# Linear attention followed by a multiplicative FFN on one core: q, k and v spread over 128 partitions, 64x64 array tiles for the small products, and a written-out order of all steps

## The chip, the core and the metric

The kernel runs on one NeuronCore of a Trainium2 chip. A core has a matrix engine (PE in the profile; PEld are its weight loads), a vector engine (DVE), an activation engine (ACT), a general engine (POOL) and a queue processor that issues DMAs (SP). The metric is the device time of one execution in microseconds (us), as the median of several runs. Smaller is better.

## What is computed

```python
# q, k, v: (8 batches, 8 heads, 576 tokens, 64); x becomes (4608 tokens, 512)
q_s = softmax(q, axis=-1)            # over the 64 channels
k_s = softmax(k, axis=2)             # over the 576 tokens
kv  = einsum('bhsd,bhse->bhde', k_s, v)      # one 64x64 matrix per head
x   = einsum('bhsd,bhde->bhse', q_s, kv)     # then heads beside each other: 4608 x 512
out = (((x @ w1) * (x @ w2)) @ w3) @ w_out   # 512 -> 1024, 1024 -> 1024 -> 512
```

Inputs and outputs are float32; the products run in float16.

## The kernel before

**Weights.** `make_w3o` casts `w_out` and `w3` to float16, transposes the blocks of `w3` on PE (line 439) and multiplies them (line 453), so that `w3 @ w_out` is one 1024x512 matrix `W3O`. `make_w12` casts `w1` and `w2` and makes the sums of their quadrants (`wc`, line 476) that the seven-product scheme below needs.

**Attention of one batch (`attention`).** k and v arrive with 64 groups of 9 tokens x 2 heads on 128 partitions, two loads of 576 KB each (line 246 issues every load). q arrives in another layout: 96 partitions of 6 tokens, pool `sq` with 2 buffers. ACT takes the exponentials (k at line 298, q at line 316). DVE sums q's rows and takes reciprocals (lines 322 and 324), POOL normalises q (line 327) and casts v (line 305). q is then transposed to `qsT`: for batches 0 and 1 on PE (line 342, copied out by DVE at line 348), for the others by a transposing DMA (line 354). The product kv runs in 64x64 array tiles, two at a time on the diagonal of the array: head i uses partitions 64i to 64i+63 and writes PSUM partitions 64i to 64i+63 (line 370, 72 matmuls of 65 columns for a batch; column 65 is the sum of k's exponentials). DVE takes reciprocals (line 377) and writes the normalised kv of two heads as a block diagonal 128x128 matrix `kv2` with two instructions (line 380). The x product is then 8 full-array matmuls of 288 columns (line 396), copied into `xt` by ACT (line 410; half of batch 0 by DVE). PSUM holds `pa` (2 banks, attention), `px` (2) and `pp` (4).

**FFN.** Tokens are cut into groups: one of 512 tokens done plainly (`plain`, lines 508, 515, 521) and five of 640, 896, 896, 896 and 768 tokens, whose two first products are done with a seven-product scheme on halves (`wino`): `t_comb` makes sums of x's quadrants on DVE (line 543), then for each of 8 blocks of 128 features there are 14 matmuls of h columns, h being half the group (line 567), three evictions by ACT (lines 588, 589), four DVE operations (line 592) and one product on POOL (line 618). `s2` multiplies by `W3O`: 8 matmuls of 512 columns for 128 tokens (line 633), evicted by ACT (line 643) or, every second time in the last group, by DVE (line 645), and stored by SP (line 657).

**What sets the order.** Every step is a task with an engine, an assumed duration, dependencies, buffers, a priority and a class. `Planner.run` plays the tasks through with the assumed durations when the program is built, picks for every engine the task that could start first (ties by class and priority), gives buffers out, and puts filler matmuls on a blank tile (line 712) where PE would stand idle in the first 65 us. The order it finds is the program order of each engine; on the chip each engine works through its list strictly in that order and waits at a step whose inputs are late.

Of the kernel before, what the change touches and what calls it, by code (L numbers as in the profile page):

```python
# [14 lines left out]

class Buf:


    def __init__(self, pool):
        self.pool, self.users, self.tile, self.left = pool, [], None, 0  # L20


class Task:
    def __init__(self, eng, dur, emit, deps, bufs, prio, cls, dma):
        self.eng, self.dur, self.emit, self.prio, self.cls, self.dma = eng, dur, emit, prio, cls, dma
        self.deps = [d for d in deps if d is not None]
        self.bufs = bufs
        self.start = self.done = None


class Fill:


    def __init__(self, op, tile, n):
        self.op, self.tile, self.n = op, tile, n

    def emit(self):
        self.op(self.tile, self.n)


class Planner:

    LAT = {"PE": 230, "ACT": 150, "DVE": 150, "POOL": 150, "SP": 60}

    def __init__(self):
        self.tasks, self.pools = [], {}
        self.filler = None

    def pool(self, name, tiles):
        self.pools[name] = [(0.0, i, t) for i, t in enumerate(tiles)]

    def add(self, eng, dur, emit, deps=(), bufs=(), prio=0.0, cls=1, dma=None):
        t = Task(eng, dur, emit, list(deps), list(bufs), prio, cls, dma)
        for b in t.bufs:
            b.users.append(t)
            b.left += 1
        self.tasks.append(t)
        return t  # L60

    def run(self):
        engines = ["PE", "ACT", "DVE", "POOL", "SP"]
        todo = {e: sorted((t for t in self.tasks if t.eng == e), key=lambda t: t.prio)
                for e in engines}
        free = {e: 0.0 for e in engines}
        asleep = {e: False for e in engines}
        dma_free = 0.0
        order = []

        def ready(t):
            r = 0.0
            for d in t.deps:
                if d.done is None:
                    return None
                r = max(r, d.done)
            need = {}
            for b in t.bufs:
                if b.tile is None:
                    need[b.pool] = need.get(b.pool, 0) + 1  # L80
            for p, n in need.items():
                have = sorted(self.pools[p])
                if len(have) < n:
                    return None
                r = max(r, have[n - 1][0])
            return r

        while any(todo.values()):
            best = None
            for e in engines:  # L90
                if not todo[e]:
                    continue
                t0 = free[e]
                cands = []
                seen = 0
                for t in todo[e]:
                    r = ready(t)
                    if r is not None:
                        cands.append((max(r, t0), t))
                    seen += 1  # L100
                    if seen >= (400 if e == "PE" else 200):
                        break
                if not cands:
                    continue
                first = min(c[0] for c in cands)

                slack = 0 if e == "PE" else 120
                now = [c for c in cands if c[0] <= first + slack]
# [5 lines left out]
                if best is None or s < best[0]:  # L114
                    best = (s, e, t)
# [630 lines left out]
```

## Time and profile before

| | |
|---|---|
| runs | 259.37, 256.09 and 259.29 us; median 259.29 |
| span of the profiled execution | 257.3 us from its first to its last instruction |
| PE busy | 234.6 us (91%) |
| DVE, ACT, POOL busy | 175.7, 151.8 and 109.4 us |
| DMA | 52.10 MB, 38.80 MB of it read from memory by the inputs |

The profile is one execution, and only its span is listed; the median of the runs lies 2.0 us above that span, for what lies around it (and for the spread of the runs). A busy PE in the profile includes the drain of each matmul, which overlaps the next one, so busy PE isn't PE at its peak: the distance from one matmul's start to the next is the better measure. The "DMA share" is the mean busy share of 16 DMA engines by packet time and can pass 1. In the groups, a line shows out<-in, shapes, the number of instructions, busy time and mean ns, and then the idle time of the engine just before them with what ended it.

### The profile page before, as it was taken

The numbers are of one execution on the slowest core, as the hardware profiler recorded it, in microseconds if no ns is written. First come the engines' busy times: TensorE is split into PE (matmuls) and PEld (weight loads), VectorE is DVE, ScalarE is ACT, GpSimd is POOL, SyncE is SP. The second block draws the span as 40 slices with busy tenths as digits, with TensorE's granted clock in tenths as the row PEclk, the third lists the DMA queues.
The fourth block names the chain that finished last, engine by engine and source line by source line (L and its number), as shares of the span: only waits on it lengthen the run. The fifth ranks groups of instructions, "written<-read, shape, count | busy, mean of one in ns | idle before, by whom it ended". The sixth has DMA issues, their size and how long they took to land.

```text
span 257.3 us, 5030 instructions
## 1 busy us (share of the span) xinstructions
PE 234.6 (91%) x1820; PEld 126.5 (49%) x1820; DVE 175.7 (68%) x331; ACT 151.8 (59%) x312; POOL 109.4 (43%) x103
## 2 busy tenths in 40 slices
PE   8999889969689989699799797999999999999991
PEld 5755644443356644444455354554444455555440
DVE  2448399958787797897988979956657464565321
ACT  1147447937678979489598696655355544444310
POOL 3025800467644678367957582713132222221200
PEclk9999999997999999799999999999999999999998
DMA  7999999999979799999999951232211313122254
GB/s 256 404 328 348 399 383 286 356 209 360 220 210 383 101 307 311 334 261 292 274 293 181 381 134 46 48 85 72 50 43 42 82 41 84 41 52 71 63 149 118
DMA packets 41945, 52.10 MB, mean 202 GB/s; under 512 B 16832, under 2 KB 27072, under 8 KB 41920
## 3 DMA queue, kind: packets, MB, share of 16 engines
q1 hardware_dynamic: 41920, 51.79, 70.0%
q8 instruction: 14, 0.23, 0.4%
q14 instruction: 11, 0.09, 0.1%
HBM read 38.80 MB, written 9.44 MB: 187 GB/s over the span
## 4 chain that ended last, share of the span: by engine, by line
PE 55%; DVE 18%; DMA 15%; ACT 5%; issue 4%; SPq 1%; DVEq 0%; ACTq 0%
PE pp L633 19%; PE px L567 16%; PE pp L567 12%; DMA st<-in_moe_w_dram 10%; DVE tt L543 4%; DMA sq<-in_q_dram 4%; DVE ds L322 4%; DVE c L592 4%; PE pp L712 4%; PE pa L396 3%; DVE kv L380 2%; DMA out_dram<-osb 2%; DVE ab L592 1%; ACT xt L410 1%; ACT eq L316 1%
## 5 line engine op out<-in xcount | busy, mean ns | idle before, releaser
L633 PE MATMUL pp<-W3O,ab 128*128 128x512 f16 x288 | 80.8, 384 | 0.3 <-DVE c L592 0.2
L618 POOL TENSOR_TENSOR ab<-c,c 128x448 f16<-128x448 f16 (+2 forms) x40 | 39.4, 985 | 81.5 <-DVE c L592 80.4
L592 DVE TENSOR_TENSOR c<-pp,u 128x448 f16<-128x448 f32 (+2 forms) x80 | 46.2, 579 | 29.5 <-ACT u L588 15.7
L327 POOL TENSOR_TENSOR eq<-eq,ds 96x768 f16<-96x768 f16 x32 | 47.1, 1487 | 33.9 <-DVE ds L324 25.6
L567 PEld LDWEIGHTS <-wc 128*128 128x128 f16 x320 | 30.6, 98 | 35.2 <-DVE tt L543 4.9
L567 PE MATMUL px<-tt,wc 128*128 128x448 f16 (+2 forms) x160 | 40.2, 339 | 3.8 <-DVE tt L543 3.6
L633 PEld LDWEIGHTS <-ab 128*128 128x128 f16 x288 | 28.2, 98 | 26.4 <-issue 2.9
L588 ACT COPY u<-px 128x448 f32<-128x448 f32 x48 | 26.0, 546 | 17.9 <-PE px L567 13.6
L643 ACT ACTIVATE osb<-pp 128x512 f32<-128x512 f32 x33 | 19.7, 614 | 25.7 <-PE pp L633 23.4
L567 PEld LDWEIGHTS <-w 128*128 128x128 f16 x240 | 23.3, 98 | 22.1 <-issue 2.3
L322 DVE TENSOR_REDUCE ds<-eq 96x12 f32<-96x768 f16 x32 | 29.6, 925 | 3.9 <-ACT eq L316 3.8
L316 ACT ACTIVATE eq<-sq 96x768 f16<-96x768 f32 x32 | 26.0, 842 | 7.9 <-DMA sq<-in_q_dram 7.9
L410 ACT CAST xt<-pa 128x288 f16<-128x288 f32 (+6 forms) x72 | 23.0, 380 | 12.6 <-PE pa L396 12.5
L592 DVE TENSOR_TENSOR c<-pp,s 128x448 f16<-128x448 f32 (+2 forms) x40 | 23.0, 578 | 8.5 <-PE pp L567 7.6
L592 DVE TENSOR_TENSOR ab<-px,c 128x448 f16<-128x448 f32 (+2 forms) x40 | 23.3, 582 | 4.3 <-PE px L567 2.0
L589 ACT COPY u<-px 128x320 f32<-128x320 f32 (+1 forms) x32 | 14.2, 452 | 12.9 <-PE px L567 8.7
L567 PE MATMUL px<-xt,wc 128*128 128x448 f16 (+2 forms) x80 | 20.2, 335 | 1.2 <-ACT u L589 1.2
L567 PE MATMUL pp<-tt,wc 128*128 128x448 f16 (+2 forms) x80 | 20.4, 336 | 0.8 <-DVE tt L543 0.5
L298 ACT ACTIVATE ek<-st 128x576 f16<-128x576 f32 x32 | 21.0, 691 | 0.0
L567 PE MATMUL pp<-xt,w 128*128 128x448 f16 (+2 forms) x80 | 20.8, 342 | 0.0
L567 PE MATMUL pp<-tt,w 128*128 128x448 f16 (+2 forms) x80 | 20.3, 336 | 0.3 <-DVE c L592 0.3
L567 PE MATMUL px<-xt,w 128*128 128x448 f16 (+2 forms) x80 | 20.0, 336 | 0.2 <-DVE ab L592 0.2
(55 smaller groups left out, 254.3 us busy)
## 6 DMA issues: line engine op xcount, KB each, us to landing
sq<-in_q_dram SPq DMA_DIRECT2D x16, 576.0 KB, 8.5
st<-in_k_dram SPq DMA_DIRECT2D x16, 576.0 KB, 7.9
st<-in_v_dram SPq DMA_DIRECT2D x16, 576.0 KB, 8.7
st<-in_moe_w_dram SPq DMA_DIRECT2D x16, 512.0 KB, 7.7
out_dram<-osb SPq DMA_DIRECT2D x24, 192.0 KB, 2.3
out_dram<-osb SPq DMA_DIRECT2D x24, 128.0 KB, 2.4
st<-in_moe_w_out_dram SPq DMA_DIRECT2D x4, 512.0 KB, 7.0
out_dram<-osb SPq DMA_DIRECT2D x24, 64.0 KB, 2.0
```

What stands on the lines that cost most here:

```text
L298: nc.scalar.activation(out=ek.tile.rearrange("p r d -> p (r d)"), in_=vk(bk.tile)[:, g], func=AF.Exp)
L316: nc.scalar.activation(out=eq.tile.rearrange("p r h d -> p h r d"), in_=vq(bq.tile)[:, o:o + 2].rearrange("p h (r d) -> p h r d", r=R), fu ...
L322: nc.vector.tensor_reduce(out=ds.tile[:, 0], axis=AX.X, op=ALU.add, in_=eq.tile.rearrange("p r h d -> p (r h) d"))
L327: nc.gpsimd.tensor_tensor(out=eq.tile.rearrange("p r h d -> p (r h) d"), in0=eq.tile.rearrange("p r h d -> p (r h) d"), in1=ds.tile[:, 1][ ...
L410: (nc.vector.tensor_copy if by_dve else nc.scalar.copy)(out=xt_buf[i].tile[:, p, lo - starts[i]:hi - starts[i]], in_=xp.tile[:, lo - base: ...
L567: nc.tensor.matmul(ps.tile[:, 0:h], lhsT=lhs(c), rhs=rhs(c), start=first and c == 0, stop=c == 1, skip_group_check=not first)
L588: return lambda: nc.scalar.copy(out=dst.tile, in_=src.tile[:, 0:h]) if h == HM else \
L589: nc.scalar.copy(out=dst.tile[:, 0:h], in_=src.tile[:, 0:h])
L592: return lambda: nc.vector.tensor_tensor(out=dst(), in0=ps.tile[:, 0:h], in1=other.tile[:, 0:h], op=op)
L618: nc.gpsimd.tensor_tensor(out=ab.tile[:, 0:h], in0=c11.tile[:, 0:h], in1=c21.tile[:, 0:h], op=ALU.mult)
L633: nc.tensor.matmul(po.tile, lhsT=ab_buf[(i, ft)].tile[:, tb * P:(tb + 1) * P], rhs=W3O[ft], start=(ft == 0), stop=(ft == N_FT - 1))
L643: nc.scalar.activation(out=osb.tile, in_=po.tile, func=AF.Copy, scale=ISC)
```

## The change

**Order.** `Planner` is gone. `Steps` numbers the 1344 tasks in the order in which the code adds them, and two lists written out by hand give everything: `ORDER`, the task numbers in order of issue (six filler entries among them, 90 matmuls in all, where there were 92), and `SLOTS`, the buffer of its pool that each use gets. No durations or priorities are left. Numbers 0 to 67 are the loads (0 to 7 `w3` and `w_out` in turn, 8 and 9 `w3`, 10 to 15 q, k, v of batch 0, 16 and 17 `w3`, 18 to 25 `w1` and `w2`, then q, k, v of batches 1 to 7). Read with this numbering, the loads now begin with 10, 6, 11, 4, 2, 8, 0 (q of batch 0 among the first); the last piece of k of batch 0 is the 17th load and the last of the two loads of `w1` and `w2` that the first feature blocks need is the 24th. Before, batch 0 was complete with the 16th load and those two with the 20th.

**Where products stand in PE's list.** Between the second half of kv of a batch and the first x product of that batch PE's list holds, for batches 0 to 7: 2, 2, 18, 21, 18, 20, 44 and 30 other entries, nearly all of them pairs of matmuls of 320 to 512 columns. Between two neighbouring entries that use the 64x64 tiles (a half of kv or a piece of x) there are at most 3 others in 20 of 53 cases. The first product of a seven-product group stands 3 to 7 entries behind the last x product that it needs.

**Attention.** q is loaded like k and v, on 128 partitions (2 heads x 64 groups of 9 tokens), from one pool `st` of 8 buffers for all loads (before: `st` 7 and `sq` 2). The exponentials write two heads side by side. q's row sums are 4 DVE instructions of 128x576 for a batch (before: 4 of 96x768), with 2 reciprocals (before: 4) and 2 normalisations of 128x1152 on POOL (before: 4 of 96x768). Only batch 0 is transposed on PE (18 transposes; before 48 for batches 0 and 1); batches 1 to 7 take two transposing DMAs each of 128x1152 (before: 24 of 96x768 for batches 2 to 7). kv and x:

```diff
-                        for r in range(RK):
-                            for i in range(2):
-                                sl = slice(64 * i, 64 * i + 64)
-                                nc.tensor.matmul(
-                                    pa.tile[sl, o:o + 65], lhsT=ek[sl, r, :],
-                                    rhs=v16[sl, g, r, 0:65], start=(r == 0), stop=(r == RK - 1))
+                for r in range(RK):
+                    for t in range(2):
+                        for j in range(2):
+                            nc.tensor.matmul(
+                                pa.tile[64 * j:64 * j + 64, t, o:o + 65],
+                                lhsT=ek[64 * t:64 * t + 64, r, j, :],
+                                rhs=v16[64 * t:64 * t + 64, r, j, 0:65],
+                                start=(r == 0), stop=(r == RK - 1))
...
+            nc.vector.reciprocal(out=rc.tile, in_=kvv[:, :, :, 64])
+            nc.vector.tensor_tensor(
+                out=kv2.tile, in0=kvv[:, :, :, 0:64], op=ALU.mult,
+                in1=rc.tile[:, :, :, None].broadcast_to([P, 2, 2, D]))
...
-                    nc.tensor.matmul(
-                        xp.tile[:, 0:HS], lhsT=kv2.tile[:, p, :],
-                        rhs=qsT.tile.rearrange("p r s -> p (r s)")[:, hh * HS:(hh + 1) * HS],
-                        start=True, stop=True)
+                    for j in range(2):
+                        for t in range(2):
+                            nc.tensor.matmul(
+                                px.tile[64 * t:64 * t + 64, j, 0:n],
+                                lhsT=kv2.tile[64 * j:64 * j + 64, t, i, :],
+                                rhs=qsT.tile[64 * j:64 * j + 64, r0:r1, 64 * t:64 * t + 64],
+                                start=True, stop=True)
+
+                def xc(i=i, px=px, g=g, o=o, n=n):
+                    nc.scalar.copy(out=xt_buf[g].tile[:, 2 * i:2 * i + 2, o:o + n],
+                                   in_=px.tile[:, :, 0:n])
```

So kv is 36 matmuls for four heads, in quads that use all four 64x64 tiles (row tiles write different PSUM banks), and `kv2` holds only the blocks that aren't zero. The x product of four heads is cut into pieces of at most 5 groups of 64 tokens (n up to 320); a piece is four matmuls in the four tiles and one ACT copy of 2n columns. There are 38 pieces, and with the 16 halves of kv PE's list enters 64x64 tiles 51 times (some stand next to each other), where the list before entered them 10 times, for kv alone. All copies of x are ACT's.

**Buffers and groups.**

```diff
-    GROUPS = [(512, 320), (1152, 448), (2048, 448), (2944, 448), (3840, 384)]
+    GROUPS = [(0, 512), (512, 640), (1152, 1024), (2176, 1024), (3200, 1024), (4224, 384)]
-    tiles("px", 2, [P, 512], F32, psum)
-    tiles("pp", 4, [P, 512], F32, psum)
-    tiles("pa", 2, [P, 512], F32, psum)
+    tiles("ps", 6, [P, 512], F32, psum)
+    tiles("pa", 1, [P, 2, 512], F32, psum)
```

The groups of tokens are now 512 (plain), 640, 1024, 1024, 1024 and 384, so h is 320, 512, 512, 512 and 192: the sum of h stays 2048, as do the 14 matmuls, 3 evictions and 5 elementwise steps of a block. All PSUM tiles of the FFN and of `w3` come from six buffers `ps`. Attention has one buffer `pa` of two banks for kv, for the transposes of batch 0 and for every piece of x. `xt` has 2 buffers (before 3), `ab` 18 (16), `osb` 4 (3). The rows of a token tile are stored by two DMAs of 64 rows each (before: one to three of 32 to 96 rows).

729 lines of the change are left out of this document (301 added, 428 removed), and 94 rows, old and new, of tables (ORDER, SLOTS).

## The prediction

> **What bounds the kernel now.** I read the head of the page first, then the table of stages, then PE's groups and waits inside the stage that loses time.
>
> ```profile
> span 257.3 us, 5030 instructions
> PE 234.6 (91%) x1820; PEld 126.5 (49%) x1820; DVE 175.7 (68%) x331; ACT 151.8 (59%) x312; POOL 109.4 (43%) x103
> ...
> PE 55%; DVE 18%; DMA 15%; ACT 5%; issue 4%; SPq 1%; DVEq 0%; ACTq 0%
> ```
>
> ```profile
> 0.00:60.00 60.00, 55.21 (x491) 32.41 (x492) 39.34 (x83) 29.87 (x46) 22.06 (x28) 0.98 1.02 329
> 60.00:160.00 100.00, 87.66 (x859) 48.22 (x858) 83.79 (x157) 78.32 (x179) 63.52 (x53) 0.98 0.96 257
> 160.00:246.00 86.00, 85.59 (x446) 43.27 (x445) 50.80 (x91) 42.45 (x86) 23.84 (x23) 1.00 0.22 60
> 246.00:257.30 11.30, 6.18 (x29) 2.62 (x27) 1.82 (x3) 1.19 (x2) 0.00 (x0) 0.94 0.50 139
> ```
>
> The columns are the stage, its length, busy time of PE, PEld, DVE, ACT and POOL, granted clock, DMA share and GB/s. PE leads the chain. From 160 us on it is full and nothing but fewer columns would help. Before, loads (share 1.02) and then everything at once (DMA 0.96, DVE 84%, ACT 78%) run beside it. How much PE loses there shows only against its real pace, which dense rows give:
>
> ```profile
> 241.66 10.52 PE L633 MATMUL pp<-W3O,ab 128*128 128x512 f16 x48
> ```
>
> ```profile
> 73.47 0.43 PE L567 MATMUL px<-xt,w 128*128 128x320 f16 x2
> 73.83 1.34 PE L370 MATMUL pa<-v,ek 64*64 64x65 f16 x72
> 75.11 0.45 PE L567 MATMUL pp<-xt,w 128*128 128x320 f16 x2
> ...
> 81.13 0.41 PE L396 MATMUL pa<-qsT,kv 128*128 128x288 f16 x2
> 81.38 0.43 PE L567 MATMUL pp<-xt,w 128*128 128x320 f16 x2
> ```
>
> Less one drain (0.38 us), 47 steps of 512 columns took 10.14 us: 0.216 us each, 0.42 ns a column, so 0.135 us for 320 columns and 0.189 for 448. Two x matmuls of 288 columns took 0.25 us (81.13 to 81.38).
>
> ```profile
> L633 PE MATMUL pp<-W3O,ab 128*128 128x512 f16 x88 | 24.7, 384 | 0.3 <-DVE c L592 0.2
> L567 PE MATMUL px<-tt,wc 128*128 128x448 f16 (+1 forms) x80 | 19.4, 337 | 3.6 <-DVE tt L543 3.6
> L396 PE MATMUL pa<-qsT,kv 128*128 128x288 f16 x50 | 11.5, 292 | 6.3 <-DVE kv L380 6.2
> ...
> L567 PE MATMUL px<-xt,wc 128*128 128x448 f16 (+1 forms) x40 | 9.9, 331 | 1.2 <-ACT u L589 1.2
> ...
> L370 PE MATMUL pa<-v,ek 64*64 64x65 f16 x432 | 8.8, 199 | 0.0
> ```
>
> ```profile
> 60.00:160.00 100.00, 57.15 (x283) 27.00 (x284) 0.98 0.96 257
> ```
>
> These are PE's groups between 60 and 160 us and the same stage for line 567 alone. At that pace the stage holds 88 x 0.216 = 19.0 us of line 633; 283 of line 567 (112 of 320 columns, the rest 448): 15.1 + 32.3; 216 pairs of kv at 0.032 (below): 7.0; 50 x 0.125 = 6.3. Sum 79.7 of 100: **PE loses 20.3 us here**, 6.2 waiting for DVE's normalised kv, 3.6 for `tt`, 1.2 for an eviction, 2 to the clock (0.98), and 7.3 in gaps too short for the list. The longest kind looks like this (DVE and PE in one wait):
>
> ```profile
> 126.11 0.89 DVE L322 TENSOR_REDUCE ds<-eq 96x12 f32<-96x768 f16 x1
> ...
> 127.03 0.22 DVE L324 RECIPROCAL ds<-ds 96x12 f32<-96x12 f32 x1
> 127.18 0.12 DVE L377 RECIPROCAL rc<-pa 128x4 f32<-128x4 f32 x1
> 127.33 0.86 DVE L380 TENSOR_TENSOR kv<-pa,rc 64x256 f16<-64x256 f32 x2
> ...
> 128.25 0.42 PE L396 MATMUL pa<-qsT,kv 128*128 128x288 f16 x2 [1.57 <-DVE kv L380]
> ```
>
> kv is ready in PSUM, but DVE first sums q (126.11), and PE's list has next to nothing between kv and x.
>
> **The change part by part: PE's own work.**
>
> ```profile
> 28.99 0.76 PE L370 MATMUL pa<-v,ek 64*64 64x65 f16 x36
> ```
>
> Against the 72 matmuls at 73.83 (1.34 us), 18 more pairs took 0.58 us: 0.032 us a pair, so 9.3 us for the 288 pairs before. The trace shows no quad. It costs at least one pair period and at most two: 144 x 0.032 = 4.6 to 9.3 us. I take 4.6, since a pair is already near the 0.027 us that its 65 columns need and its second tile shows no price: -4.7. The Trainium skill (TensorE: Matmul & The Clock Gate, Part 3, The mechanism) gives a pack one matmul's duration plus about 4 ns for each further tile; by it a quad is 8 ns dearer than a pair, 1.2 us more in all, which no run here shows yet.
>
> x was 64 x 0.125 = 8.0 us. The 38 pieces have 9216 columns: 3.9 us if four tiles run at once, 7.8 if two do. By the pair, 3.9: -4.1.
>
> Entering the small tiles costs. The two matmuls at 73.47 have streamed by 73.74, kv starts at 73.83: 0.09 us. Its 36 pairs have streamed by 74.99, the next full matmul starts at 75.11: 0.12. A visit costs 0.21 us, and 51 visits instead of 10 make +8.6 (nothing where PE would wait anyway, so 0 to 8.6; taken whole). The Trainium skill (TensorEngine Tiling (Array Packing), Key Properties) says that a change of tiling mode drains TensorE; the trace agrees, with these 0.21 us, and by it most of what the four tiles give is handed back.
>
> Fewer PE transposes: 48 x 96 less 18 x 128 columns: -1.0. **PE's work: -4.7 - 4.1 + 8.6 - 1.0 = -1.2 us**, between -9.8 and +7.4. So the small tiles alone move the end little.
>
> **The start.**
>
> ```profile
> 0.00:37.00 37.00, 34.28 (x321) 22.54 (x322) 19.75 (x41) 15.39 (x24) 13.00 (x21) 1.00 1.00 352
> ```
>
> ```profile
> 36.97 0.59 PE L508 MATMUL px<-xt,w 128*128 128x512 f16 x2
> ...
> 55.88 0.76 PE L370 MATMUL pa<-v,ek 64*64 64x65 f16 x36 [1.28 <-POOL v L305]
> 57.31 0.43 PE L342 MATMUL pa<-ident,eq 96*128 96x96 f16 x6 [0.67 <-POOL eq L327]
> ```
>
> Until the first feature block (36.97) PE waits for loads at 352 GB/s, so what PE saves there is worth nothing. The weights of that block come with the 24th load (13.0 MB) instead of the 20th (10.9 MB): 2.2 MB or 6 us later, against a margin of up to 6 (10.9 MB have landed by about 31 us). 0 to +6; I take +2, as copying and casting eat part of the margin. The waits at 55.88 and 57.31 (1.95 us) belong to batch 1, whose PE transposes go and whose kv stands later in the list: -1.5.
>
> **The stage from 60 to 160 us.** From batch 2 on PE's list has 18 or more other entries between kv and x, at least 18 x 0.27 = 4.9 us, against a DVE chain of 2.1 us (126.11 to 128.25): the 6.2 go, less 0.7 for stragglers: -5.5. The first product of a group stands 3 to 7 entries behind its last x, the first that needs `tt` further on: -3 of the 4.8 of `tt` and eviction. Fewer long gaps bring the clock back: -1.5 of 2. DVE, ACT and POOL also get less to do:
>
> ```profile
> L327 POOL TENSOR_TENSOR eq<-eq,ds 96x768 f16<-96x768 f16 x32 | 47.1, 1487 | 33.9 <-DVE ds L324 25.6 <-DVE rc L377 3.3 <-ACT xt L410 1.9
> L322 DVE TENSOR_REDUCE ds<-eq 96x12 f32<-96x768 f16 x32 | 29.6, 925 | 3.9 <-ACT eq L316 3.8
> L316 ACT ACTIVATE eq<-sq 96x768 f16<-96x768 f32 x32 | 26.0, 842 | 7.9 <-DMA sq<-in_q_dram 7.9
> L298 ACT ACTIVATE ek<-st 128x576 f16<-128x576 f32 x32 | 21.0, 691 | 0.0
> L643 ACT ACTIVATE osb<-pp 128x512 f32<-128x512 f32 x33 | 19.7, 614 | 25.7 <-PE pp L633 23.4 <-DVE ab L592 2.3
> L410 ACT CAST xt<-pa 128x288 f16<-128x288 f32 x48 | 18.5, 416 | 10.4 <-PE pa L396 10.3
> L324 DVE RECIPROCAL ds<-ds 96x12 f32<-96x12 f32 x32 | 7.2, 224 | 1.1
> L380 DVE TENSOR_TENSOR kv<-pa,rc 64x256 f16<-64x256 f32 x16 | 6.8, 422 | 0.4
> ```
>
> Row sums of 576 instead of 768 columns: between 694 (in proportion) and 925 ns, I take 710: -6.9 us. Half the reciprocals: -3.6. One kv instruction for two: -3.4. DVE thus loses some 14 us (4 without the shorter sums to 17), most of it in this stage. POOL: 16 of 1487 x 1.5 = 2230 ns for 32 of 1487: -11.9, and 0 if each took twice as long. ACT: 32 x (842 - 691) = -4.8, and about as much by fewer, longer copies of x, at 416 ns for 288 columns and 614 for 512. None of these sets the end; they shorten what PE waits for, and I count half of the 7.3 us of short gaps: -3.6 (0 to -7.3). **Stage: -13.6**, between -8 and -19.
>
> The end stays: PE's last matmul, an eviction and a store, 5 us, and one more `osb` buffer changes nothing on PE.
>
> **Sum:** 257.3 - 1.2 + 2 - 1.5 - 13.6 = 243.0 us span; with the 2.0 us by which the median lies above this span, **245 us**. Its own range, from the stage (-8 to -19) and the start (0 to +6), is 239 to 251.
>
> **The rivals.** *The list leaves no gap (239 us).* If the 20.3 us fall to 2 and the start costs nothing: 257.3 - 1.2 - 1.5 - 18.3 + 2 = 238.3, about 239. For it: every wait named has cover. Against it: the list is fixed and can't give way to a late transfer.
>
> *Tiles run two at a time (254 us).* kv and x back at pair cost: +4.7 + 3.9 on 245. The trace shows only tiles that share neither rows nor columns of the array; quads share both. The second tile of a pair being free speaks against it.
>
> *DMA sets the pace (253 us).*
>
> ```profile
> 60.00:150.00 90.00, 78.96 (x748) 43.38 (x747) 75.36 (x141) 70.47 (x164) 58.87 (x49) 0.97 1.02 275
> ```
>
> ```profile
> qsT<-eq SPq DMA_TRANSPOSE x24, 6.7
> ```
>
> At 352 GB/s the 24.8 MB of these 90 us need 70; the other 21.5 us of DMA time are transposes and q's shorter pieces, at most 1 us for each of some 22. After it 14 transposes of twice the size cost 14 (by number) to 28 us (by size). Left after 37 us are 25.8 MB of inputs (73 us) and some 3 MB of stores (9): the last load lands between 133 and 147 us. PE's list reaches kv of batch 7 at about 141 by my sum (118 us of columns, 7 of visits, 16 of start). At the late end, with 3 us for cast and exponentials, it waits 9 less a little: 253.
>
> *The single `pa` (slower: 268 us).* PE writes a piece of x, ACT copies up to 640 columns (about 0.7 us by the slope of the copies), and only then may PE write the next, with 48 uses of the one buffer in a row; before there were two and more. In 20 of 53 neighbouring entries at most 3 others stand between; two of them cover 0.86 us. If an exponential (0.69 us) runs ahead of the copy, the handover takes 1.4 us: 0.5 lost, 48 times, +24. From 0.3 us a handover on, it eats the whole gain. For it: ACT is 78% busy in this stage. Against it: the written lists place copies and products for each other.
>
> **How the numbers follow.** Forecast 0.48, no gaps 0.20, pairs 0.10, DMA 0.12, single `pa` 0.10 (half of it mild, around today's time). A measurement of this kernel can tell about 2% from no change: below 254.1 is faster. Faster: 0.47 + 0.20 + 0.06 + 0.07 = 0.80; within 2%: 0.01 + 0.04 + 0.04 + 0.05 = 0.14; slower: the rest, 0.06. The range, 235 to 257, takes in the better case and the two middle ones and leaves out most of the single `pa`.
>
> **What would show it.** Right: PE's idle before x (line of the x product) under 1 us in all; kv quads every 0.03 to 0.04 us; about 0.2 us around each visit; first feature block at 37 to 40 us; PE's end 5 us before the span's; row sums near 0.7 us. Wrong: PE idle before x released by ACT's copy (single `pa`); PE waiting for casts of v or exponentials of k of batches 5 to 7 (DMA); quads at 0.06 us (pairs); or the first feature block beyond 43 us.

## The result, and the profile after

| | before | after |
|---|---|---|
| median (lowest to highest of 4 runs) | 259.33 (256.09 to 260.12) us | 244.55 (243.95 to 245.5) us |
| span of the profiled execution | 257.3 us | 243.3 us |
| ratio after / before | | 0.9481, 95% interval 0.94 to 0.9562 |

Ratios here are taken over fast executions alone, so they need not equal the ratio of the medians, and e11's times leave out one slow execution (257.28 us, at a granted clock of 0.96). Beside the experiments the kernel before read 259.1 to 260.1 us, so differences of medians below 1 us are not read.

The forecast was 245.0 us, from a span of 243.0. The head of the page and the chain of waits of the kernel after:

```profile
span 243.3 us, 4956 instructions
PE 228.0 (94%) x1876; PEld 114.5 (47%) x1876; DVE 155.7 (64%) x293; ACT 146.2 (60%) x280; POOL 96.0 (39%) x85
PE 56%; DMA 25%; ACT 6%; DVE 4%; POOL 3%; issue 2%; SPq 2%; ACTq 0%; DVEq 0%; POOLq 0%
```

PE still leads the chain. DVE's part fell from 18% to 4%, and DMA's rose from 15% to 25%: 9% of the span are transposing DMAs, which the chain before did not hold, and the other 16% are loads. The table of stages, in the same columns as before:

```profile
0.00:60.00 60.00, 52.51 (x478) 29.21 (x478) 34.82 (x63) 30.91 (x51) 17.67 (x21) 1.00 1.00 340
60.00:160.00 100.00, 96.82 (x952) 45.42 (x952) 77.86 (x149) 78.14 (x151) 59.29 (x44) 1.00 0.92 256
160.00:236.00 76.00, 76.00 (x438) 38.84 (x437) 42.32 (x83) 35.94 (x78) 19.01 (x21) 1.00 0.34 74
236.00:243.30 7.30, 2.68 (x13) 1.00 (x11) 0.69 (x1) 1.19 (x2) 0.00 (x0) 0.94 0.66 145
```

The stage from 60 to 160 us has PE busy 96.82 of 100 us instead of 87.66, at a clock of 1.00 instead of 0.98. The stage ahead of it has it busy less than before (52.51, was 55.21). PE's groups in the middle stage:

```profile
L550 PE MATMUL ps<-tt,wc 128*128 128x512 f16 (+1 forms) x134 | 33.6, 351 | 0.1
L616 PE MATMUL ps<-W3O,ab 128*128 128x512 f16 x109 | 28.7, 380 | 0.0
...
L466 PE MATMUL pa<-qsT,kv 64*64 64x256 f16 (+3 forms) x100 | 7.7, 297 | 2.2 <-DMA qsT<-eq 2.0 <-DVE kv L439 0.2
L429 PE MATMUL pa<-v,ek 64*64 64x65 f16 x432 | 5.6, 194 | 0.6 <-POOL v L365 0.6
```

Line 550 (567 before) makes the seven products, 616 (633) the last product, 466 (396) x, 429 (370) kv. The wait before x fell from 6.3 us to 2.2, and it is the transposing DMA that ends it, no longer DVE's kv; the 3.6 us of `tt` are 0.1. At the same paces as in the prediction (512 columns 0.216 us, 320 columns 0.135, quads of kv 0.0346) this stage holds 88.1 us of columns, where before it held 79.7. PE thus loses 11.9 us here, was 20.3, though it now enters the small tiles 35 times in it, was 6 times.

A visit to the small tiles, and the start and the end:

```profile
90.64 1.04 PE L616 MATMUL ps<-W3O,ab 128*128 128x512 f16 x4
91.60 0.48 PE L429 MATMUL pa<-v,ek 64*64 64x65 f16 x36
92.01 0.45 PE L550 MATMUL ps<-tt,w 128*128 128x320 f16 x2
```

```profile
39.02 1.90 PE L309 MATMUL ps<-ab,ab 128*128 128x512 f16 x8
40.76 0.59 PE L494 MATMUL ps<-xt,w 128*128 128x512 f16 x2
```

```profile
235.71 2.97 PE L616 MATMUL ps<-W3O,ab 128*128 128x512 f16 x13
```

The four matmuls at 90.64 have streamed by 91.50, and kv starts at 91.60: 0.10 us. Nine quads of 0.0346 us are through by 91.91, and the next full matmul starts at 92.01: 0.10. The first feature block (line 494) starts at 40.76, was 36.97. PE ends at 238.68, 4.6 us before the span's end.

Four marks, each a start time in PE's timeline (the span is the page's), show where kernels part. "First `tt` product" is the first matmul that reads `tt`; the fifth column is the time from there to the last matmul's start, so the steady part alone.

| us | first block | first `tt` product | last matmul | steady part | span | median |
|---|---|---|---|---|---|---|
| before | 37.0 | 67.9 | 251.8 | 183.9 | 257.3 | 259.33 |
| after | 40.8 | 69.5 | 238.3 | 168.8 | 243.3 | 244.55 |
| e2, kv late | 39.2 | 69.7 | 239.9 | 170.2 | 244.9 | 246.44 |
| e3, steps in the planner's way | 39.1 | 70.7 | 246.9 | 176.2 | 252.3 | 254.15 |
| e4, more work for DVE and POOL | 39.4 | 70.0 | 241.3 | 171.4 | 246.3 | 248.02 |
| e6, other start | 37.6 | 67.1 | 235.5 | 168.4 | 240.5 | 242.95 |
| e7, batch 1 by PE | 39.4 | 70.3 | 238.5 | 168.2 | 244.1 | 245.94 |
| e8, more visits | 40.9 | 70.8 | 247.8 | 177.1 | 252.8 | 254.31 |
| e10, e6 and kv halves of batches 4 to 7 adjacent | 37.7 | 67.3 | 235.3 | 168.0 | 240.6 | 242.43 |
| e1, x in the full array | 42.6 | 79.6 | 245.6 | 165.9 | 250.6 | 251.59 |
| e9, that and e10's start | 42.0 | 79.5 | 245.5 | 166.0 | 250.5 | 251.89 |
| e11, e10 with halved weight loads | 42.8 | 81.8 | 249.0 | 167.3 | 254.0 | 254.57 |
| e12, e9 with whole weight loads | 37.2 | 67.0 | 233.4 | 166.4 | 238.4 | 240.49 |

From before to after the steady part gave 15.1 us, the tail 0.5, and the start took 1.6 back. The theory was the prediction's: the list, and not the small tiles, makes the gain. Its rivals: the list's cover for kv alone, the lighter DVE and POOL, the small tiles themselves.

### The profile page after: what moved, and what is told of

It reads as the page before. It is cut to its first block, busy times and chain, and to the rows that moved or that the text cites. A ratio compares the mean times of both kernels' runs of the same rounds, so it can differ in the third digit from the quotient of the medians.

```text
span 243.3 us, 4956 instructions
## 1 busy us (share of the span) xinstructions
PE 228.0 (94%) x1876; PEld 114.5 (47%) x1876; DVE 155.7 (64%) x293; ACT 146.2 (60%) x280; POOL 96.0 (39%) x85
## 4 chain that ended last, share of the span: by engine, by line
PE 56%; DMA 25%; ACT 6%; DVE 4%; POOL 3%; issue 2%; SPq 2%; ACTq 0%; DVEq 0%; POOLq 0%
PE ps L550 32%; PE ps L616 22%; DMA qsT<-eq 9%; DMA st<-in_q_dram 6%; DMA st<-in_moe_w_dram 4%; DMA st<-in_k_dram 3%; DMA st<-in_moe_w_out_dram 3%; POOL eq L390 3%; SPq L233 2%; PE pa L466 2%; ACT uu L571 2%; ACT eq L376 1%; ACT ek L355 1%; DVE cc L574 1%; ACT osb L626 1%
## 5 line engine op out<-in xcount | busy, mean ns | idle before, releaser
L574 DVE TENSOR_TENSOR cc<-ps,uu 128x512 f16<-128x512 f32 (+2 forms) x120 | 66.9, 577 | 36.9 <-PE ps L550 16.8
L571 ACT COPY uu<-ps 128x512 f32<-128x512 f32 (+2 forms) x120 | 57.3, 505 | 38.8 <-PE ps L550 34.9
L616 PE MATMUL ps<-W3O,ab 128*128 128x512 f16 x288 | 76.2, 380 | 0.0
L601 POOL TENSOR_TENSOR ab<-cc,cc 128x512 f16<-128x512 f16 (+2 forms) x40 | 39.1, 982 | 76.6 <-DVE cc L574 76.0
L550 PE MATMUL ps<-tt,wc 128*128 128x512 f16 (+2 forms) x240 | 56.6, 337 | 0.1
L390 POOL TENSOR_TENSOR eq<-eq,ds 128x1152 f16<-128x1152 f16 x16 | 34.8, 2173 | 34.8 <-DVE ds L387 16.7
L550 PE MATMUL ps<-xt,w 128*128 128x512 f16 (+2 forms) x160 | 38.6, 337 | 0.3
L380 DVE TENSOR_REDUCE ds<-eq 128x9 f32<-128x576 f16 x32 | 23.5, 744 | 16.5 <-ACT eq L376 16.4
L355 ACT ACTIVATE ek<-st 128x576 f16<-128x576 f32 x32 | 20.6, 688 | 14.8 <-DMA st<-in_k_dram 14.8
L376 ACT ACTIVATE eq<-st 128x576 f16<-128x576 f32 x32 | 21.3, 686 | 11.5 <-DMA st<-in_q_dram 10.2
L574 DVE TENSOR_TENSOR ab<-ps,cc 128x512 f16<-128x512 f32 (+2 forms) x40 | 22.8, 576 | 6.6 <-PE ps L550 5.5
L473 ACT CAST xt<-pa 128x512 f16<-128x512 f32 (+4 forms) x38 | 21.5, 565 | 6.3 <-PE pa L466 6.1
L550 PE MATMUL ps<-xt,wc 128*128 128x512 f16 (+2 forms) x80 | 20.3, 337 | 0.0
L494 PE MATMUL ps<-xt,w 128*128 128x512 f16 x64 | 14.8, 379 | 0.9 <-ACT cc L501 0.9
L668 PE MATMUL ps<-blank 128*128 128x256 f16 x90 | 13.6, 317 | 1.1 <-DVE blank L660 1.1
```

The lines of the kernel that those rows point to most:

```text
L355: nc.scalar.activation(out=ek.tile[:, :, j, :], func=AF.Exp, in_=vk(bk.tile)[:, j].rearrange("p (r d) -> p r d", r=RK))
L376: nc.scalar.activation(out=eq.tile[:, :, j, :], func=AF.Exp, in_=vq(bq.tile)[:, j].rearrange("p (r d) -> p r d", r=RK))
L380: nc.vector.tensor_reduce(out=ds.tile[:, 0, j], axis=AX.X, op=ALU.add, in_=eq.tile[:, :, j, :])
L390: nc.gpsimd.tensor_tensor(out=eq.tile, in0=eq.tile, op=ALU.mult, in1=ds.tile[:, 1].rearrange("p j r -> p r j")[:, :, :, None].broadcast_to ...
L473: nc.scalar.copy(out=xt_buf[g].tile[:, 2 * i:2 * i + 2, o:o + n], in_=px.tile[:, :, 0:n])
L550: nc.tensor.matmul(ps.tile[:, 0:h], lhsT=lhs(c), rhs=rhs(c), start=first and c == 0, stop=c == 1, skip_group_check=not first)
```

## The experiments: where the gain comes from

**e3: the same steps, ordered by the old planner's rules.** Only the two lists differ (144 filler matmuls instead of 90).

```diff
 ORDER = [
-    ('ps', 2, 27), 10, 6, 11, 4, 2, 8, 0, 142, 144, 96, 145, 97, ('ps', 2, 29), 151, 153, 152, 3, 98, 88,
+    0, ('ps', 1, 38), 1, 2, 3, 4, 5, 6, 7, 72, 73, 8, ('ps', 2, 11), 68, 74, 9, 80, 75, ('ps', 3, 4), 81,
...
```

> The same steps, tiles, layouts, groups and buffers as the changed kernel, in the order and with the buffers that the planner of the kernel before finds with its rules, priorities and assumed durations (kv and x pieces at 0.48 us and at n/2.4 ns plus 0.11). Theory (the written-out order is what fills PE between 60 and 160 us): most of the gain goes, 251 to 258. Rivals (tiles or layouts carry the gain): 244 to 248.

Measured 254.15 us (253.08 to 255.16), ratio to before 0.9844 (0.975 to 0.994): 9.6 us over the kernel after. PE's timeline and the stage's x group of this kernel:

```profile
97.64 1.89 PE L618 MATMUL ps<-W3O,ab 128*128 128x512 f16 x8
105.06 0.38 PE L468 MATMUL pa<-qsT,kv 64*64 64x192 f16 x4 [5.53 <-DMA qsT<-eq]
106.20 0.43 PE L468 MATMUL pa<-qsT,kv 64*64 64x256 f16 x4 [0.76 <-ACT xt L475]
```

```profile
L468 PE MATMUL pa<-qsT,kv 64*64 64x256 f16 (+3 forms) x104 | 8.4, 313 | 7.1 <-DMA qsT<-eq 5.5 <-ACT xt L475 1.4
```

With everything but the order as in the kernel after, the waits before x are 7.1 us again, more than the 6.3 of before, and PE stands still for 5.53 us at 99.5 us for a transposing DMA. Behind that wait the granted clock (third number from the end) is 0.50:

```profile
105.06:110.70 5.64, 4.19 (x23) 1.43 (x24) 4.45 (x7) 4.20 (x8) 0.00 (x0) 0.50 1.03 224
```

PE works 4.19 of these 5.64 us, and at half the clock that costs some 2.1 us more. So this one wait makes about 7.6 us, next to a difference of 9.0 between the two spans (1.2 of it by the first `tt` product, 7.4 in the steady part). The 1.4 us ended by ACT's copy are the single `pa` of the rival, in small. So of the 14.8 us, about 9.6 hang on the order, in this set of steps; but they are the distance to one planned list, which mainly has one transfer too late, and not the sum of many small gaps. A planned list with other assumed times for the transposing DMAs was not tried.

**e2: kv late.** In batches 2 to 7 kv stands two PE entries ahead of its x, as batches 0 and 1 have it.

```diff
-    tiles("ek", 3, [P, RK, 2, D])
+    tiles("ek", 6, [P, RK, 2, D])
...
-    tiles("kv2_", 2, [P, 2, 2, D])
-    tiles("rc", 2, [P, 2, 2], F32)
+    tiles("kv2_", 3, [P, 2, 2, D])
+    tiles("rc", 3, [P, 2, 2], F32)
```

> The changed kernel with kv and its normalisation of batches 2 to 7 moved in the lists to two PE entries before the first x product of the same batch, as close as batches 0 and 1 have it (6 buffers for k's exponentials instead of 3, so that nothing else has to wait for the later kv). Theory (the cover between kv and x is a good part of the gain): cover falls from 5 to 17 us to about 0.9, against 1.2 to 1.7 us for PE's last column, a DVE instruction already running, the reciprocal and the multiplication: 0.4 to 0.9 us lost six times, +2.5 to +5, about 248. Rivals (four tiles, or the relief of the other engines, carry the gain): no change, 244 to 245.

Measured 246.44 us (244.19 to 246.69): +1.9, less than the theory's low end. The stage's x group, its longest wait, and kv of a moved batch (DVE and PE):

```profile
L467 PE MATMUL pa<-qsT,kv 64*64 64x256 f16 (+3 forms) x92 | 7.2, 302 | 3.7 <-DMA qsT<-eq 3.5
```

```profile
64.54 0.30 PE L467 MATMUL pa<-qsT,kv 64*64 64x256 f16 x4 [2.74 <-DMA qsT<-eq]
...
122.54 0.94 PE L430 MATMUL pa<-v,ek 64*64 64x65 f16 x72
...
123.55 0.18 DVE L439 RECIPROCAL rc<-pa 128x4 f32<-128x4 f32 x1 [0.62 <-PE pa L430]
...
123.77 0.42 DVE L440 TENSOR_TENSOR kv<-pa,rc 128x256 f16<-128x256 f32 x1
...
124.39 0.33 PE L467 MATMUL pa<-qsT,kv 64*64 64x320 f16 x4
```

Without the cover PE still doesn't wait for kv (DVE ends no wait before x here): DVE stands ready when kv's last column comes (it waits 0.62 us for it), where at 126.11 us in the trace of before it was still summing q. So the distance in PE's list was one of two protections, and taking away one cost little. The move also puts the two halves of kv side by side, 47 visits in the trace instead of 51, which can hide up to 0.8 us of its cost. The wait that grew, for the transposing DMA, is not what the move cost: 2.74 us of it stand in batch 1, which was not moved, and the first `tt` product is no later for it (69.7 and 69.5 us). The 1.4 us that the steady part lost have no single wait behind them.

**e4: more work for DVE and POOL.** Half of q's row sums and half of the casts of v run twice; nothing else differs.

```diff
+                    if j == 1:
+                        nc.vector.tensor_reduce(out=ds.tile[:, 0, j], axis=AX.X, op=ALU.add,
+                                                in_=eq.tile[:, :, j, :])
...
+                if i == 0:
+                    nc.gpsimd.tensor_copy(
+                        out=v16.tile[:, :, :, 0:D].rearrange("p r j d -> p j r d"),
+                        in_=vv(bv.tile).rearrange("p j (r d) -> p j r d", r=RK))
```

> The changed kernel with half of q's row sums done twice (16 x 0.744 = 11.9 us more of DVE) and half of v's casts done twice (8 x 1.19 = 9.5 us more of POOL), which gives back about what the new layout saved on both; the results are the same numbers. Theory (these engines are covered and only lengthen short gaps): +0 to +4, 244.5 to 248.5. Rival (their relief carries the gain): +8 to +14, 253 to 258.

Measured 248.02 us (247.93 to 248.17): +3.5 for 12.0 us more on DVE and 9.3 on POOL. Groups of this kernel (the added ones are 387 and 369):

```profile
L387 DVE TENSOR_REDUCE ds<-eq 128x9 f32<-128x576 f16 x16 | 12.0, 752 | 0.5
L369 POOL CAST v<-st 128x1152 f16<-128x1152 f32 x8 | 9.3, 1166 | 0.5
```

DVE is then 86% busy in the middle stage, and the steady part is 2.6 us longer. So 21.3 us of work on engines that the chain of waits hardly names cost 3.5. The list was not arranged anew for it.

## The experiments: the start

**e6: the first 40 us listed anew.** `w3` and `w_out` come first, and the two loads of `w1` and `w2` that the first blocks need are the 17th and 18th (the 23rd and 24th in the kernel after).

```diff
 ORDER = [
-    ('ps', 2, 27), 10, 6, 11, 4, 2, 8, 0, 142, 144, 96, 145, 97, ('ps', 2, 29), 151, 153, 152, 3, 98, 88,
+    0, ('ps', 1, 30), 1, 2, 3, 4, 5, 6, 7, 72, 73, 10, ('ps', 2, 14), 68, 74, 11, 80, 75, ('ps', 3, 6),
...
```

> The changed kernel with its first 40 us listed anew: w3 and w_out load first, as in the kernel before, the first quarter of w1 and w2 moves from the 23rd and 24th load to the 17th and 18th, and the steps of w3, w_out and batch 0 follow that; all later steps keep their sequence on each engine. Theory (the late weights cost the start 2 to 4 us): the first feature block begins at 37 to 39 us instead of 40.8 and the whole takes 241 to 243. Rival (PE's work before the first block is covered either way, and what gates the group behind it is batch 1): 244 to 246, whatever the first block does.

Measured 242.95 us (242.32 to 243.89). PE's timeline of this kernel:

```profile
37.61 0.59 PE L495 MATMUL ps<-xt,w 128*128 128x512 f16 x2
```

The first block starts 3.1 us earlier, the first `tt` product 2.4, the median is 1.6 lower, as the theory had it: the late start was a cost of the change. The edit moves the steps of `w3`, `w_out` and batch 0 along with the loads (and has 111 filler matmuls for 90), so the loads are not tried alone.

**e7: batch 1 transposed on PE.** The kernel after waits for transposing DMAs in batch 1; this takes them away (the two lists take in its steps).

```diff
-        attention(b, b < 1)
+        attention(b, b < 2)
```

> The changed kernel with batch 1 transposed on PE again (18 transposes more, two transposing DMAs fewer). PE waits 0.9 and 1.3 us there for qsT of batch 1 (at 58 and 64 us), and the two DMAs take some 4 us of all DMA engines in the stage in which loads are late. Theory (this is what holds up the first seven-product group): that group begins 1.5 to 3 us earlier, and the whole takes 242 to 243.5. Rival (loads of batches 1 and 2 gate it anyway): 244 to 245.5.

Measured 245.94 us (244.83 to 246.47): no gain, and a little above the range of the rival. The groups with waits between 40 and 75 us, first of the kernel after, then of this one:

```profile
L494 PE MATMUL ps<-xt,w 128*128 128x512 f16 x64 | 14.8, 379 | 0.9 <-ACT cc L501 0.9
L466 PE MATMUL pa<-qsT,kv 64*64 64x256 f16 (+2 forms) x28 | 2.1, 292 | 1.8 <-DMA qsT<-eq 1.8
L429 PE MATMUL pa<-v,ek 64*64 64x65 f16 x144 | 1.8, 194 | 0.6 <-POOL v L365 0.6
```

```profile
L495 PE MATMUL ps<-xt,w 128*128 128x512 f16 x62 | 14.4, 379 | 2.0 <-DVE ab L508 2.0
L467 PE MATMUL pa<-qsT,kv 64*64 64x256 f16 (+2 forms) x24 | 1.8, 286 | 1.2 <-DVE kv L440 0.7 <-DVE qsT L408 0.6
L403 PE MATMUL pa<-ident,eq 128*128 128x128 f16 x18 | 1.3, 218 | 1.0 <-ACT xt L474 1.0
```

3.3 us of waits became 4.2, with other names on them: the wait for the DMA (1.8) went, and DVE's `ab`, kv and `qsT` and ACT's copy took its place. So taking away the wait that the list named gained nothing here: other inputs were as late.

**e10: e6 with the two kv halves of batches 4 to 7 next to each other**, which leaves 47 visits of 51 in the trace (only `ORDER` and `SLOTS` differ: the entry of the first half moves to just ahead of the second). Batch 0 was meant too, but its halves stay apart, at 26.03 and 27.41 us.

> The run that begins with w3 and w_out, with the two halves of kv of batches 0 and 4 to 7 put beside each other in PE's list, so that PE visits the small tiles 46 instead of 51 times. Theory (0.21 us a visit): -1.0 us, 241.5 to 242.5 against 243.0. Rival (drains hide): 243.0.

Measured 242.43 us (241.97 to 243.24), ratio 0.9429 (0.937 to 0.949). That is 0.5 below e6, with a span no shorter (240.6 and 240.5): four visits less are not told apart from nothing. It is the lowest median of a kernel that computes the task; e12 below does not.

## The experiments: what the small tiles cost

**e8: more visits.** Each of the 38 pieces of x is split by a full-array matmul of 16 columns.

```diff
+                        if j:
+                            nc.tensor.matmul(px.tile[:, 1, 0:16], lhsT=blank[:, 0:P],
+                                             rhs=blank[:, 0:16], start=True, stop=True)
```

> The changed kernel with a full-array matmul of 16 columns (on a blank tile, overwritten right after) between the two row halves of every piece of x, so that each of the 38 pieces visits the small tiles twice, two tiles at a time. Theory (a visit drains PE for 0.21 us): 38 x 0.21 = 8.0 us for the visits, 3.8 because two tiles run instead of four, 0.3 for the 16 columns: about +12 where PE has no slack, 253 to 257. Rival (a drain lasts but hides in what PE waits for anyway): +4, 247 to 249.

Measured 254.31 us (253.82 to 254.6), ratio 0.9878 (0.979 to 0.997): +9.8, in the theory's range. One piece:

```profile
150.09 0.33 PE L469 MATMUL pa<-qsT,kv 64*64 64x320 f16 x2
150.34 0.18 PE L466 MATMUL pa<-blank 128*128 128x16 f16 x1
150.45 0.33 PE L469 MATMUL pa<-qsT,kv 64*64 64x320 f16 x2
150.71 0.60 PE L553 MATMUL ps<-xt,w 128*128 128x512 f16 x2
```

From its start to the next full matmul it takes 0.62 us, where a whole piece of this size takes 0.26 (156.24 to 156.50 in e10, below). Added up in this way, the 38 pieces take 12.5 us more than in the kernel after. Of these, 3.9 us are not visits: 9216 columns of 0.42 ns run a second time because two tiles work instead of four; the 16 columns are another 0.3. That leaves 8.3 us, 0.22 for each added visit. Of the 12.5 us, 9.8 reach the end: about four fifths of what a visit adds is paid, and the rest hides.

**e1, e5, e9: x in the full array.** x goes back to 128x128 block diagonals, so that only kv enters the small tiles. The halves of a feature block then come from other heads, so that something has to be loaded in another order: in e1 and e9 the heads of q, k and v (in loads of the same size) and the rows of `w1` and `w2` (two DMAs of 64 partitions and 256 KB for each of 512 KB), in e5 q, k and v alone, as below. e9 has e10's start and adjacent halves.

```diff
-            nc.vector.tensor_tensor(
-                out=kv2.tile, in0=kvv[:, :, :, 0:64], op=ALU.mult,
-                in1=rc.tile[:, :, :, None].broadcast_to([P, 2, 2, D]))
+            for j in range(2):
+                sl = slice(64 * j, 64 * j + 64)
+                nc.vector.tensor_tensor(
+                    out=kv2.tile[sl, :, :, sl], in0=kvv[sl, :, :, 0:64], op=ALU.mult,
+                    in1=rc.tile[sl, :, :, None].broadcast_to([64, 2, 2, D]))
...
-                    for j in range(2):
-                        for t in range(2):
-                            nc.tensor.matmul(
-                                px.tile[64 * t:64 * t + 64, j, 0:n],
-                                lhsT=kv2.tile[64 * j:64 * j + 64, t, i, :],
-                                rhs=qsT.tile[64 * j:64 * j + 64, r0:r1, 64 * t:64 * t + 64],
-                                start=True, stop=True)
+                    for t in range(2):
+                        nc.tensor.matmul(
+                            px.tile[:, t, 0:n], lhsT=kv2.tile[:, t, i, :],
+                            rhs=qsT.tile[:, r0:r1, 64 * t:64 * t + 64],
+                            start=True, stop=True)
...
-             src[b, 4 * i:4 * i + 4].rearrange("(j t) (g r) d -> (t g) j (r d)", t=2, r=RK))
+        ws = src[bt, 4 * i:4 * i + 4].rearrange("(t j) (g r) d -> j t g (r d)", t=2, r=RK)
...
+            for j in range(2):
+                nc.sync.dma_start(out=b.tile[:, j * RK * D:(j + 1) * RK * D], in_=ws[j])
```

> The changed kernel with the x product on the full array: kv2 is block diagonal again (two DVE instructions write it), a piece of x is two matmuls of n columns over all 128 rows, and only kv enters the small tiles (the heads are paired so that the rows of w1 and w2 come in two DMAs of 64 partitions for each load). Theory (a visit to the small tiles drains PE for 0.21 us, so the four tiles give x nothing): 38 visits x 0.21 = -8.0 us, columns 7.7 instead of 3.84 us = +3.8, so PE saves 4.1 us; DVE pays 3.4 us more. Expected about 240.5 us, 239 to 243. Rival (the four tiles carry the gain of the change): x is back at its old price, +4 us, about 248.5. Rival (layouts relieve DVE, POOL and DMA, and PE's work doesn't matter): 244 to 246.

> The x product on the full array again, as in the run before, but without the halved weight loads that held up that run's start (its first seven-product group began 10 us late, and took 165.9 instead of 168.8 us from there to PE's last matmul): heads are paired so that w1 and w2 load whole, and each load of q, k and v is issued as two DMAs of 128 partitions. Theory (a visit costs PE 0.21 us and x gains nothing from the four tiles): -4 us on PE from the first group on, the start as in the changed kernel, SP with 48 more issues of some 0.45 us: 241 to 243. Rival (the four tiles carry part of the gain): 247 to 249, and from the first seven-product group to PE's last matmul no less than 168.8.

> The full-array x product of the first run (heads paired anew, w1 and w2 in halves of 64 partitions) with the first 40 us listed as in the run that begins with w3 and w_out, and the two halves of kv of every batch beside each other in PE's list. Theory (x gains nothing from the four tiles; only the late weights spoiled the first run): PE saves 3 to 4 us from the first seven-product group on against that start run's 243.0, and 1 us for five visits less: 238 to 241. Rival (the four tiles carry part of the gain): 243 or more, with no less than 168 us from that group to PE's last matmul.

Measured: e1 251.59 us (250.73 to 253.59), e5 711.57 (711.21 to 712.37), e9 251.89 (250.22 to 252.6). None came out as the theory had it. In e1 and e9 the steady part is indeed shorter (165.9 and 166.0 us), but the first `tt` product comes 10 to 12 us late. e5 is set by its loads, which moved 74 GB/s over the span:

```profile
DMA packets 41303, 52.67 MB, mean 74 GB/s; under 512 B 18240, under 2 KB 22336, under 8 KB 41280
```

It says nothing of x. e9 starts as e10 does and is as late as e1, so the order of the start isn't the cause; that leaves the loads and the full array itself.

**e11 and e12: the halved loads without the full array, and the full array without the halved loads.**

```diff
-        load(("w12", wi, qt), P * 4096, 388.0, lambda t: t[:, :1024].rearrange("p (c f) -> p c f", c=4),
-             w.rearrange("(c p) f -> p c f", p=P)[:, :, qt * 256:(qt + 1) * 256])
+        ws = w.rearrange("(c j e) f -> j e c f", j=2, c=4)
...
+            for j in range(2):
+                nc.sync.dma_start(
+                    out=b.tile[64 * j:64 * j + 64, :1024].rearrange("p (c f) -> p c f", c=4),
+                    in_=ws[j, :, :, qt * 256:(qt + 1) * 256])
```

That is e11's edit on e10; e12 is e9 with whole loads again. In e12 each half of a block meets the weight rows of other heads, so it leaves out the right pairing and does not compute the task; its steps, sizes and columns are e9's, and only its time counts.

> The version of 242.43 us (the start relisted, the kv halves adjacent, x in four 64x64 tiles) with one edit: each quarter of w1 and w2 is loaded by two DMAs of 64 partitions and 256 KB instead of one of 128 partitions and 512 KB. The two kernels with a full-array x had these halved loads too, and reached the first product of `tt` at 79.5 us instead of 67.3. Theory: the halved loads cost them that, by their lower rate (between 40 and 60 us they moved 256 GB/s, the version with whole loads 351). Then this kernel too has its first block near 42 us, the first `tt` product at 76 to 80 us, 168 us from there to the last matmul, and takes 251 to 255 us. Rival: the full-array x or its order of heads, and with it the wait for the zeroed kv tiles, cost them the start. Then nothing changes here: 242 to 244 us.

> The full-array x with the start relisted and the kv halves adjacent (251.89 us), with the loads of w1 and w2 whole again, 512 KB on 128 partitions in the order of the kernel after. In that order each half of a block of features meets the w1 and w2 rows of other heads: part of the computation is changed (x, its sizes and all steps are the same), so that only the time counts. Theory: with the start no longer spoiled, what is left is the full-array x against the four tiles: 38 visits of 0.21 us less (-8.0), the full array's streaming back (+4.1, as it was counted for the change), so some 2 to 4 us less than the version of 242.43: 238.5 to 240.5 us, the first `tt` product at 67 to 68 us and 164 to 166 us from there to the last matmul. Rival: the full-array x itself delays the start: first `tt` product near 79 us and about 250 us. Second rival: outside the start it gains nothing: 242 to 243.5 us.

Measured: e11 254.57 us (253.23 to 256.12), e12 240.49 (239.93 to 241.42), ratios to before 0.9789 (0.973 to 0.985) and 0.9263 (0.922 to 0.930). Both follow the theory, e11 with its first `tt` product a little beyond the numbers (81.8 us) and e12 at the upper edge of its own. The DMA issues of `w1` and `w2` (KB each, median us to landing) and the stage from 40 to 60 us, for e11, then for e10:

```profile
st<-in_moe_w_dram SPq DMA_DIRECT2D x16, 256.0 KB, 12.0
...
40.00:60.00 20.00, 14.07 (x55) 5.20 (x54) 9.74 (x20) 8.64 (x15) 2.14 (x1) 0.83 1.09 225
```

```profile
st<-in_moe_w_dram SPq DMA_DIRECT2D x16, 512.0 KB, 10.2
...
40.00:60.00 20.00, 17.18 (x151) 7.43 (x149) 16.86 (x34) 14.36 (x24) 7.97 (x5) 1.00 1.10 351
```

Half the bytes take longer to land (e10's 16 issues take in eight of `w3`, which e11 lists apart). The DMA engines are as busy in both stages (1.09 and 1.10) and move 225 instead of 351 GB/s, all loads together. The packets of `w1` and `w2` are 1 KB in both; between 20 and 60 us the trace has them at 88 ns each in e11 and 51 in e10. Why 64 partitions make them slower, no run shows. It costs e11 14.5 us at the first `tt` product, with x untouched; a granted clock of 0.83 instead of 1.00 in this stage is part of that.

What the full array is worth is read from two pairs with equal weight loads: e12 against e10 is 1.9 us faster, e9 against e11 2.7. One piece of x in each, first e10's, then e12's:

```profile
155.28 1.03 PE L551 MATMUL ps<-tt,wc 128*128 128x512 f16 x4
156.24 0.33 PE L467 MATMUL pa<-qsT,kv 64*64 64x320 f16 x4
156.50 0.60 PE L617 MATMUL ps<-W3O,ab 128*128 128x512 f16 x2
```

```profile
154.39 1.02 PE L551 MATMUL ps<-tt,wc 128*128 128x512 f16 x4
155.25 0.43 PE L468 MATMUL pa<-qsT,kv 128*128 128x320 f16 x2
155.52 0.60 PE L617 MATMUL ps<-W3O,ab 128*128 128x512 f16 x2
```

Less the four full matmuls ahead (4 x 0.216), the four tiles take 0.36 us of PE for 320 tokens of four heads, the full array 0.27, twice the columns and no visit. That is 0.09 for a piece of 320 columns, and more for a smaller one, since the visit stays and the streaming shrinks: 38 x 0.21 less 9216 columns of 0.42 ns is 4.1 us for the change's x product in small tiles.

## Why the prediction was right, step by step

- **PE's own work (-1.2).** kv quads: 4.6 us forecast, 144 x 0.0346 = 5.0 measured, against 9.3 before. The 0.0346 is the mean over nine quads, whose first gap is longer (0.052); 18 quads in a row (from 56.41 us) follow each other every 33.4 ns, and so do 18 pairs in a row in the kernel before (from 30.98). So a quad in a row costs what a pair does, as forecast. The rule of the Trainium skill (TensorE: Matmul & The Clock Gate, Part 3, The mechanism) puts a quad 8 ns above a pair; the four matmuls of a quad do start 3 to 4 ns apart here, but the distance from quad to quad does not grow by it. x: four tiles run at once, as taken (320 columns in 0.26 us from the piece at 156.24 to the next full matmul, 0.135 of streaming and the way out; two by two it would be 0.27 without any way out). The visit: 0.20 us at 91.60, 0.21 forecast, and e8 shows that about four fifths of what it adds is paid. So the step holds: the tiles as a set bring next to nothing, kv in quads gains 4.3 less some visits, x in small tiles loses 2 to 3.
- **The start (+2, bounds 0 to +6).** The first block came 3.8 us later, and e6 took 3.1 of it away by another order of the loads and of the steps that hang on them. Right in its mechanism, mis-sized by 1.8, and outside the 37 to 40 us that were named; by the first `tt` product 1.6 were left.
- **The waits of batch 1 (-1.5).** Not gained as named: the waits at 55.88 and 57.31 went, and 3.3 us of others stand between 40 and 75 us, with 1.8 us for the transposing DMA. The statement that PE's idle before x would be under 1 us failed by this: 2.2 us in the middle stage, all but 0.2 of them for the transposing DMA, a wait for which the sum had no term.
- **The stage (-13.6).** Without the visits PE lost 20.3 - 6 x 0.21 = 19.0 us here, and loses 11.9 - 35 x 0.21 = 4.6: -14.4. Part by part: kv -6.2 + 0.2, `tt` and eviction -4.7, clock -2 (forecast 5.5, 3 and 1.5), +2.0 for the DMA, and the rest, -3.7, in short gaps (3.6). The gain from the cover was given the right size for another reason than cover alone: e2 takes it away and pays 1.9, e3 takes the whole order away and pays 9.6, most of it in one late transfer.
- **Less work for DVE and POOL (-3.6).** e4 puts 12.0 and 9.3 us back and pays 3.5. That agrees in size; that the gain lay in short gaps, as forecast, is argued from the sum above and not shown. Row sums, normalisation, reciprocals and kv:

```profile
L390 POOL TENSOR_TENSOR eq<-eq,ds 128x1152 f16<-128x1152 f16 x16 | 34.8, 2173 | 34.8 <-DVE ds L387 16.7 <-ACT W3O L317 12.5 <-ACT osb L626 4.7
L380 DVE TENSOR_REDUCE ds<-eq 128x9 f32<-128x576 f16 x32 | 23.5, 744 | 16.5 <-ACT eq L376 16.4
L387 DVE RECIPROCAL ds<-ds 128x18 f32<-128x18 f32 x16 | 3.9, 251 | 0.0
L439 DVE TENSOR_TENSOR kv<-pa,rc 128x256 f16<-128x256 f32 x8 | 3.4, 424 | 0.3
```

  744 ns for 710 forecast, 2173 for 2230, 3.9 us for 3.6, 3.4 for 3.4. DVE lost 20.0 us in all, not 14: its row sums, reciprocals and kv gave 12.8, its sums for `tt` another 4.6 (17.6 to 13.0, below), which the forecast left out, and smaller steps the rest.
- **The rivals.** Tiles two at a time: excluded by the quads. The single `pa`: no wait before x is ended by ACT's copy in the kernel after; in e3 1.4 us are, so it hangs on the list. DMA's pace: a wait for transposes, 2.0 us, not the 9 of the loads. No gaps (239): 11.9 us are still lost in the stage, 7.3 of them in visits.
- **The sum.** That 243.0 us met 243.3 is partly luck. By the first `tt` product the start cost 1.6 us, where +2 and -1.5 make 0.5; the steady part gave 15.1, where 1.2 and 13.6 make 14.8; and the tail, forecast unchanged, gave 0.5.

What stays open: why e12 gains 1.9 us and not the 4.1 that its pieces save (DVE, which writes kv in two instructions there, is busier in the middle stage, 81.4 against 77.8 us in e10, but that it costs the rest isn't shown); how much of the order's 9.6 us another planned list would lose; and how much lies in the loads' order and how much in PE's.

## What to carry to other kernels

Price an array mode by what it costs to enter it, too: here 36 matmuls in a visit of 0.5 us paid for the entry, four of 256 columns did not. When the steps of a dense stage are changed, try the order as an edit by itself, since the same steps in two orders were 9.6 us apart, and then look for the one long wait before crediting many small ones. And before a layout is judged, compare the rate of its loads in GB/s at equal DMA share; two kernels here had their first `tt` product 10 and 12 us late with a load shape that had been thought free.

## What the runs showed of the hardware

- With weight loads cut from 128 partitions and 512 KB to two of 64 partitions and 256 KB, all loads together moved 225 GB/s instead of 351 at the same DMA share between 40 and 60 us, and a 1 KB packet of these weights took 88 ns instead of 51 (e11, e10).
- After a wait of PE of 5.53 us the granted clock was 0.50 until 110.70 us (e3), and after one of 2.74 us it was 0.50 from 64.8 to 68.2 (e2).
- q, k and v loaded with two groups of 64 rows as the outer pattern brought the whole program to 74 GB/s (e5), where the kernel after moves 217.
- Half of DVE's sums for `tt`, those that read x alone, take 591 ns on average in the groups of 640, 1024 and 384 tokens, where they took 1120 in the groups of 640, 896 and 768; the other half took about as long as before. The cause wasn't tried. The rows, before and after:

```profile
L543 DVE TENSOR_TENSOR tt<-xt 128x896 f16<-128x896 f16 (+2 forms) x10 | 10.9, 1120 | 3.2 <-ACT xt L410 3.2
```

```profile
L529 DVE TENSOR_TENSOR tt<-xt 128x1024 f16<-128x1024 f16 (+2 forms) x10 | 5.8, 591 | 1.8 <-ACT xt L473 1.8
```
